# Strassen products for seven pairs of tiles, gated loads, another tile order and masks on VectorE in a fused attention and feed-forward kernel

## The chip, the cores and the metric

The kernel runs on one core of a Trainium2 chip. The metric is the device time of one execution in microseconds (us); the lower, the better. Times are medians of the runs of one batch. A run more than 1.5% above the fastest run of the same kernel is put down as slow and left out of the ratios.

## The reference

Local attention with a few global keys feeds a two-layer network. The shapes are batch 4, 8 heads, 768 positions, head size 64; 8 global keys and a local window of 96; model width 512, hidden width 2048.

```python
scores = scale * q @ k.T                              # per batch and head
keep = (key < 8) | ((rel >= 0) & (rel < 96))          # rel = query - key
dist = 96 where global and not local, else abs(rel)
a = softmax(where(keep, scores - slope[h] * dist, -1e9))
x = (a @ v) as [3072, 512]                            # heads side by side
h = x @ w_in                                          # [3072, 2048]
g = h - tanh(h)
out = g @ w_out                                       # [3072, 512], float32
```

Scores outside the local window vanish, so a tile of 128 queries needs its own 128 keys, the 128 before them and the 8 global ones. There are 4 x 6 = 24 tiles.

## The kernel before

A planner written in Python runs a list scheduling with assumed durations and fixes the order of the instructions on each engine before the kernel is built. It decides order only. At run time each instruction still waits for its real inputs, so a plan that guesses a landing too early makes an engine stand still at an instruction whose data is not there.

The first four tiles go alone, the other twenty in ten pairs. Work on one tile: keys and queries are turned on TensorE for the first tiles and by the crossbar transpose of the DMA engines later; scores (`a_S`), exponential on ScalarE (`a_E`), mask multiply on VectorE (`a_M`), attention times values (`a_AV`), normalisation on VectorE (`a_R`), another transpose, first layer (`m1`), tanh on ScalarE, subtraction on VectorE (`m1_g`), second layer (`m2`), eviction on ScalarE, store.

The parts that the change and the argument touch (cuts marked by `...`):

```python
tiles = [(u % B, u // B) for u in range(NU)]          # one tile of each batch in turn
...
def a_R(u, a):                                        # normalise, VectorE only
    ...
    nc.vector.reciprocal(rd, t[:, :, Dh : Dh + 1])
    nc.vector.tensor_tensor(out=x, in0=t[:, :, 0:Dh], in1=rd.to_broadcast([P, NP, Dh]), op=ALU.mult)
...
def m2(g, t, qq):                                     # 4 x 4 matmuls of 512 columns a tile
    ...
    for f in range(qq * 4, qq * 4 + 4):
        nc.tensor.matmul(o, gg[:, f, t * P : (t + 1) * P], w_out_bf[f // FJ][:, f % FJ, :],
                         start=(f == 0), stop=(f == CF - 1))
...
# identity and the distance maps on GpSimd, in its queue between the loads
pl.op(("dist", 1), POOL, 1.1, lambda e: build_dist(1), after=[("issue", ("ld", "k", 2))], pri=-2)
pl.op(("dist", 2), POOL, 1.1, lambda e: build_dist(2), after=[("issue", ("in", 1))], pri=-1.5)
pl.op(("ident",), POOL, 0.6, lambda e: make_identity(nc, ident), after=[("issue", ("ld", "k", 1))], pri=-3)
...
# the plan holds a load of tile u >= 6 back behind a block of the first layer (in the plan only)
go = [kk for a, kk in prog if a <= u - AHEAD - EARLIER] if u >= 6 else []
pl.op(key, POOL, 0.88, ..., after=[prev and ("issue", prev), go[-1] if go else None], dma=T_LD)
...
# all DMAs in one line; a crossbar transpose counts as landed 0.5 us later than another
d0 = max(dma_free, end + (1.2 if eng is SP else 1.5))
dma_free = d0 + o["dma"]
done[key] = dma_free + 0.7 + o["lag"]                 # lag=0.5 for the transposes
```

The softmax here doesn't subtract the row's maximum and nothing guards it: scores larger than these inputs give would overflow.

## Time and profile before

| quantity | before | how to read it |
|---|---|---|
| time | 217.93 us (217.9 to 218.61, 3 runs) | whole execution |
| span in the profile | 216.6 us (of another run, 218.34 us) | first to last instruction |
| TensorE busy | 205.0 us, 95% | not yet "at its peak": listed lengths overlap (a block of eight first-layer matmuls is listed at 1.04 us and takes 0.87) |
| VectorE / ScalarE busy | 60% / 57% | room for work moved off TensorE |
| useful TensorE work | 194.2 us | worked out in the prediction |

### The profile page before, as it was taken

The numbers are of one execution on the slowest core, as the hardware profiler recorded it, in microseconds if no ns is written. First come the engines' busy times: TensorE is split into PE (matmuls) and PEld (weight loads), VectorE is DVE, ScalarE is ACT, GpSimd is POOL, SyncE is SP. The second block draws the span as 40 slices with busy tenths as digits, with TensorE's granted clock in tenths as the row PEclk, the third lists the DMA queues.
The fourth block names the chain that finished last, engine by engine and source line by source line (L and its number), as shares of the span: only waits on it lengthen the run. The fifth ranks groups of instructions, "written<-read, shape, count | busy, mean of one in ns | idle before, by whom it ended". The sixth has DMA issues, their size and how long they took to land.

```text
span 216.6 us, 5328 instructions
## 1 busy us (share of the span) xinstructions
PE 205.0 (95%) x2095; PEld 143.9 (66%) x2121; DVE 130.1 (60%) x296; ACT 124.1 (57%) x244; POOL 69.8 (32%) x90
## 2 busy tenths in 40 slices
PE   8667999999999999999999999999999999999994
PEld 5446989455867857676676677667677667666643
DVE  2385868530797977777668568568557557333310
ACT  2694768422968576546745745745745745443421
POOL 7996356473625606331441341340000000000000
PEclk9999999999999999999999999999999999999999
DMA  9999999999999998999999999999523411201112
GB/s 126 125 146 195 188 200 184 182 148 165 236 132 160 182 150 129 142 146 149 124 149 159 116 118 144 114 142 134 108 65 77 111 39 49 73 3 48 48 48 97
DMA packets 111016, 27.34 MB, mean 126 GB/s; under 512 B 103696, under 2 KB 108048, under 8 KB 110992
## 3 DMA queue, kind: packets, MB, share of 16 engines
q0 software_dynamic: 77024, 13.37, 87.3%
q1 hardware_dynamic: 33968, 13.64, 33.6%
q8 instruction: 16, 0.26, 0.5%
q14 instruction: 8, 0.07, 0.1%
HBM read 27.26 MB, written 6.29 MB: 155 GB/s over the span
## 4 chain that ended last, share of the span: by engine, by line
PE 78%; DMA 15%; POOL 3%; issue 2%; ACT 0%; POOLq 0%
PE bank L339 33%; PE bank L382 33%; DMA qT<-qb 6%; DMA qb<-in_q_dram 5%; PE bank L282 5%; DMA w_in_bf<-in_moe_w_in_dram 3%; PE bank L303 2%; PE bank L301 2%; PE bank L362 2%; POOL vb L452 1%; PE bank L326 1%; POOL kb L452 1%; POOL qb L452 1%; POOL rmat L238 0%; POOL rmat L241 0%
## 5 line engine op out<-in xcount | busy, mean ns | idle before, releaser
L339 PE MATMUL bank<-xT,w_in_bf 128*128 128x256 bf16 (+1 forms) x896 | 97.6, 257 | 0.2 <-DVE xT L272 0.2
L382 PE MATMUL bank<-w_out_bf,g 128*128 128x512 bf16 x342 | 87.4, 379 | 1.5 <-issue 0.2
L542 ACT ACTIVATE th<-bank 128x512 f32<-128x512 f32 x96 | 56.2, 609 | 55.1 <-PE bank L339 50.8
L339 PEld LDWEIGHTS <-w_in_bf 128*128 128x128 bf16 x896 | 75.0, 98 | 17.5 <-issue 0.2
L348 DVE TENSOR_TENSOR g<-bank,th 128x512 bf16<-128x512 f32 x96 | 64.1, 687 | 31.7 <-ACT th L542 31.3
L382 PEld LDWEIGHTS <-g 128*128 128x128 bf16 x368 | 35.2, 98 | 28.3 <-DVE g L348 0.4
L452 POOL DMA_DIRECT2D kb<-in_k_dram x23 | 20.5, 891 | 50.5 <-DMA kT<-kb 25.4
L287 ACT ACTIVATE pd<-bank 128x512 bf16<-128x512 f32 x48 | 26.1, 601 | 8.4 <-PE bank L282 8.3
L452 POOL DMA_DIRECT2D qb<-in_q_dram x23 | 20.3, 882 | 17.8 <-DMA qT<-qb 3.9
L292 DVE TENSOR_TENSOR pd<-pd,mk 128x1024 bf16<-128x1024 bf16 x24 | 16.6, 692 | 13.6 <-ACT pd L287 13.5
L270 ACT COPY ot<-bank 128x512 f32<-128x512 f32 (+2 forms) x25 | 14.4, 574 | 18.1 <-PE bank L382 12.1
L452 POOL DMA_DIRECT2D vb<-in_v_dram x24 | 21.3, 890 | 5.1 <-PE bank L303 2.2
L287 ACT ACTIVATE po<-bank 128x512 bf16<-128x512 f32 x40 | 22.1, 622 | 0.0
L313 DVE TENSOR_TENSOR x<-bank,rden 128x256 bf16<-128x256 f32 x48 | 20.4, 425 | 1.7
L292 DVE TENSOR_TENSOR po<-po,mk 128x1024 bf16<-128x1024 bf16 x20 | 13.8, 692 | 5.2 <-ACT po L287 5.2
L282 PEld LDWEIGHTS <-kT 64*128 64x128 bf16 x352 | 10.1, 94 | 8.2 <-issue 7.8
L282 PE MATMUL bank<-qT,kT 64*128 64x128 bf16 x352 | 14.0, 217 | 0.6 <-DMA qT<-qb 0.5
L301 PE MATMUL bank<-vb,pd 128*128 128x65 bf16 x192 | 14.0, 193 | 0.1
L301 PEld LDWEIGHTS <-pd 128*128 128x128 bf16 x192 | 12.5, 97 | 2.1 <-DVE pd L292 0.4
L303 PE MATMUL bank<-vb,po 128*128 128x65 bf16 x160 | 12.4, 193 | 0.0
L303 PEld LDWEIGHTS <-po 128*128 128x128 bf16 x160 | 10.4, 97 | 1.7
L317 DVE COPY kT<-kT 128x32 bf16<-128x32 bf16 x16 | 4.5, 282 | 9.1 <-PE bank L282 8.8
(38 smaller groups left out, 73.6 us busy)
## 6 DMA issues: line engine op xcount, KB each, us to landing
out_dram<-ot SPq DMA_DIRECT2D x23, 256.0 KB, 3.3
vb<-in_v_dram POOLq DMA_DIRECT2D x24, 128.0 KB, 6.2
kb<-in_k_dram POOLq DMA_DIRECT2D x23, 128.0 KB, 7.3
qb<-in_q_dram POOLq DMA_DIRECT2D x23, 128.0 KB, 7.2
w_in_bf<-in_moe_w_in_dram POOLq DMA_DIRECT2D x4, 512.0 KB, 10.1
w_out_bf<-in_moe_w_out_dram POOLq DMA_DIRECT2D x4, 512.0 KB, 13.1
kT<-kb SPq DMA_TRANSPOSE x18, 5.7
qT<-qb SPq DMA_TRANSPOSE x18, 5.4
```

Of the source, the lines that this page charges most:

```text
L270: nc.scalar.copy(out=dst, in_=src)
L282: nc.tensor.matmul(t[hh][:, p * P : (p + 1) * P], kt[r, p, :], qt[r, p, :], start=True, stop=True)
L287: nc.scalar.activation(dst, t, AF.Exp, bias=0.0, scale=scale)
L292: nc.vector.tensor_tensor(out=p, in0=p, in1=mk[:, m, :, :], op=ALU.mult)
L301: nc.tensor.matmul(o, pd[:, slot(h), :], vd[:, h, :], start=True, stop=w is None)
L303: nc.tensor.matmul(o, buf("po", ("p", u, 1))[:, slot(h), :], bufs[vname(w)][got["vb", w]][:, h, :], start=False, stop=True,)
L313: nc.vector.tensor_tensor(out=x, in0=t[:, :, 0:Dh], in1=rd.to_broadcast([P, NP, Dh]), op=ALU.mult)
L339: nc.tensor.matmul(t[:, (f - f0) * n : (f - f0 + 1) * n], w_in_bf[j][:, c, fo : fo + P], xt[:, c, 0:n], start=(c == 0), stop=(c == CD - 1),)
L348: nc.vector.tensor_tensor(out=dst, in0=t.rearrange("q (b n) -> q b n", n=n), in1=th.rearrange("q (b n) -> q b n", n=n), op=ALU.subtract,)
L382: nc.tensor.matmul(o, gg[:, f, t * P : (t + 1) * P], w_out_bf[f // FJ][:, f % FJ, :], start=(f == 0), stop=(f == CF - 1),)
L452: pl.op(key, POOL, 0.88, lambda e, u=u, src=src, dst=dst: nc.gpsimd.dma_start(out=dst(), in_=rows(src, u)), after=[prev and ("issue", prev ...
L542: pl.op(("th", g, f), ACT, 0.55, lambda e, g=g, f=f: nc.scalar.activation(buf("th", ("th", g, f)), buf("bank", ("h", g, f)), AF.Tanh, bias ...
```

## The change

Its intent is to take work from TensorE, which is full. Seven pairs do the second layer by Strassen's scheme: seven half-size products in place of eight, at the price of sums on VectorE. The rest makes room for that and mends the plan.

```diff
+    FAST = set(range(6, 13))              # the pairs done by Strassen
+    def a_sum(e, g, kk):                  # 5 sums of 128x1024 bf16 a pair, VectorE
+        add(e, buf("hb", ("a", g, kk)), gblk(...), sign, gblk(...))
+    def product(g, kk):                   # one of seven: 8 matmuls of 256 columns
+        for f in range(CH):
+            ...
+            nc.tensor.matmul(o, a, b, start=(f == 0), stop=(f == CH - 1))
     ... ten sums of the output weights once; five steps of recombination a pair (s34 t u cx ab cs)
-    tiles = [(u % B, u // B) for u in range(NU)]
+    TILES = [(0, 0), (0, 1), (1, 0), (1, 1), (1, 2), (3, 0), ...]   # a batch's tiles follow each other
+    R_ENGS = [(ACT, 0.7), (DVE, 0.36)]    # normalisation may go to ScalarE, in 4 pieces of 64
     ... copies of the global keys and values too
-    pl.op(("ident",), POOL, 0.6, lambda e: make_identity(nc, ident), ...)
-    pl.op(("dist", 1), POOL, 1.1, ...)
+    pl.op(("rel",), POOL, 0.45, lambda e: build_rel(), ...)          # one iota
+    pl.op(("ident",), DVE, 0.2, ... tensor_scalar(out=ident, in0=rel, ... is_equal))
+    pl.op(("dist", 1), DVE, 0.6, ...)     # the maps from the iota, on VectorE
+                if go:
+                    gates[key] = go[-1]   # the gate becomes a real wait of the load
-              after=[("ld", nm, u), go], ..., dma=T_TR, lag=0.5)
+              after=[("ld", nm, u), go], ..., dma=T_TR, lag=LATE)    # LATE = 2.0
     ... the plan's DMA model: two rings that share the engines, in place of one line
+    arrive = "q1 k1 q2 v0 q3 k2 q0 v1 v2 i0 k3 i1 v3 i2 i3 v6 k5 v5 ...".split()
+    pl.op(("touch",), ACT, 0.5, ... dma_start(out=touch, in_=w_in_r[:, :, 0:16]))  # early small read
```

A gate is the block of the first layer behind which the plan holds a load back; from now on the load really waits for it. A bank is one of the eight pieces of the memory that TensorE writes its results to.

Some smaller edits came with these: keys and queries of seven tiles in place of six are turned on TensorE, and attention outputs of six in place of eight; values are stored 96 wide in place of 65; the scores of a tile are planned as two pieces; the lead of loads over the first layer in the plan is 4.5 tiles in place of 4.0; limits hold back how many banks each layer may take.

## The prediction

> **What bounds the kernel now.** I read the occupancy slices first, then the chain of waits, then the groups of instructions, and last the timelines of single engines, because a busy share alone would mislead here.
>
> ```profile
> span 216.6 us, 5328 instructions
> PE 205.0 (95%) x2095; PEld 143.9 (66%) x2121; DVE 130.1 (60%) x296; ACT 124.1 (57%) x244; POOL 69.8 (32%) x90
> PE   8667999999999999999999999999999999999994
> DVE  2385868530797977777668568568557557333310
> PEclk9999999999999999999999999999999999999999
> DMA  9999999999999998999999999999523411201112
> PE 78%; DMA 15%; POOL 3%; issue 2%; ACT 0%; POOLq 0%
> ```
>
> The reader is to see a TensorE that is full from the fifth slice (about 21 us) to the end at full clock, with VectorE at five to seven tenths beside it. DMA is busy for three quarters of the run, but its 15% of the chain lies mostly in the first 30 us. Whether "full" is also back to back is answered by the chain of waits in the middle of the run:
>
> ```profile
> 103.33 0.81 PE bank L382 x3
> 104.14 0.55 PE bank L282 x16
> 104.69 0.98 PE bank L339 x8
> 105.67 0.86 PE bank L382 x4
> 106.53 0.87 PE bank L339 x8
> 107.41 0.86 PE bank L382 x4
> ```
>
> The columns are start, length and work. Eight first-layer matmuls 256 wide take 0.87 us, four second-layer matmuls 512 wide 0.86 us, sixteen score matmuls 0.55 us, and each piece starts where the last ended. So the middle is bound by TensorE's issue rate, and only work taken from TensorE there shortens the run. The start is different (timeline of TensorE, then of GpSimd):
>
> ```profile
> 17.50 0.40 PE L326 MATMUL bank<-ident,kb 128*128 128x128 bf16 x4 [2.38 <-DMA kb<-in_k_dram]
> 17.73 1.06 PE L339 MATMUL bank<-xT,w_in_bf 128*128 128x128 bf16 x16
> 9.03 0.78 POOL L422 DMA_DIRECT2D w_in_bf<-in_moe_w_in_dram  x1
> ```
>
> The first weight block is issued at 9.03 and landed 7.54 us later, at 16.6 (chain of waits). The first matmul that uses it starts only at 17.73, because four transposes of a key tile stand ahead of it in the queue and their load lands at 17.50.
>
> Useful TensorE work of the kernel before, at issue intervals read from the trace: first layer 640 x 0.109 + 256 x 0.0557 = 84.0; second layer 368 x 0.2165 + last tile 3.5 = 83.2; scores 352 x 0.0345 = 12.1; attention times values 352 x 0.0295 = 10.4; transposes 80 x 0.056 = 4.5. Sum 194.2 us. Of the 217.9 us measured, some 24 us are therefore no useful matmul: 9.5 us waiting for first data between 5.1 and 17.7, 5.1 us before that, some 5 us of small gaps after 17.7, and about 4 us of last evictions, store and launch.
>
> **What the Trainium skill says.** (1) "TensorE: Matmul & The Clock Gate", section "Wait — 56ns, not 53.3ns?": warm matmuls start N / 2.4 GHz plus about 2.5 ns apart. For N = 256 that is 109 ns; the trace agrees (0.87 us for eight). Cutting a 512-wide matmul into two 256-wide ones thus costs almost nothing, and seven products instead of eight are a real eighth less. (2) "VectorE: DVE Perf Modes", section "The perf-mode tier table (the rule you actually need)": a two-tensor operation runs at 2x for bf16 in SBUF and at 1x with a PSUM or float32 operand. The trace agrees: 1024 bf16 elements take 692 ns, 512 float32 from PSUM 687 ns. (3) "Perfetto Trace Analysis", section "Optimizing Scalar/DVE Operations": the listed latency of an instruction is longer than the time it holds the engine. The trace agrees: six subtractions of 687 ns each took 3.67 us in a row, 0.60 us apart. I count VectorE by these distances: 0.60 for the subtraction, 0.61 for a mask multiply, 0.34 for a normalisation half, 0.19 for its reciprocal. (4) "ScalarE: Activation LUTs", section "What ACT_TABLE_LOAD costs": 186 ns plus 0.833 ns per element, 93 ns more for a pointer operand, 93 ns overlap. For 64 elements with a pointer scale that is 0.24 us apiece (an estimate from that page; no instruction of the kernel before has this form).
>
> **The change, part by part.** *Strassen.* Seven of the ten pairs of tiles do their second layer in seven products of eight 256-wide matmuls: 7 x 7 x 8 x 0.109 = 42.7 us in place of 14 x 16 x 0.2165 = 48.5 us. TensorE work falls by 5.8 us, to 188.4. All of it lies in the bound part, so it is the certain gain if nobody else holds TensorE up.
>
> What it costs VectorE: per pair five sums of 128x1024 bf16 (5 x 0.61), and for recombination one 256-wide SBUF sum (0.28, estimated from the 0.34 with PSUM), one 256-wide with PSUM (0.34), two 512-wide with PSUM (1.2) and one 512-wide in SBUF (0.58): 5.45 us. Seven pairs make 38, and ten once-only sums of the output weights 6. In return 27 of the 48 normalisation halves and 10 of the 16 value copies go to ScalarE in the built order, about 9 + 2 us. VectorE goes from 60% to some 75% of the span. ScalarE gains 108 small pieces x 0.24 = 26 us and loses 14 evictions of 0.5 us.
>
> An average is not enough, so I counted the tight stretch in the built order: VectorE from the first Strassen sum to the last reciprocal of attention. It holds 28 sums (17.1), 43 subtractions (25.8), 24 masks (14.6), 26 reciprocals (4.9), 12 normalisation halves (4.1), 25 recombinations (12.0), 11 small copies (2.6): 81 us. TensorE's order over the same stretch (from the first-layer block that feeds that sum to the last attention matmul) holds 45 blocks of 0.87 (39.2), 35 products (30.5), scores 6.6, attention 6.1 and second layer 4.3: 86.8 us. ScalarE has 46 tanh (25.3), 48 exponentials (23.5), 56 pieces (13.4) and some 5 of copies: 67 us. So TensorE stays the longest, but VectorE is at 94% in strict order. I charge 2 us for bubbles over about ten tiles.
>
> *Start.* GpSimd makes one iota (0.3) in place of the identity and two masks before the first weight issue (about 1.4 us in the chain of waits), but eight loads now precede the weights in its queue, where seven did (0.88 more). The issue comes about 0.2 us earlier. The small early read of the weights on ScalarE's queue may take a first-access delay off: between 12 and 13 us DMA's share drops to 0.87 from about 2, so I guess 0.5. More certain: first-layer matmuls now stand right behind the weights instead of behind the key transposes, and 17.73 can become about 16.1, 1.6 us. Before it stand 0.7 us more of attention work than before (32 score and 32 value matmuls, against 24 and 16). Together 2.2 us.
>
> *Gates and late landings in the plan.* In the trace before, TensorE waits for a crossbar transpose twice, 0.2 and 0.3 us (the long DMA pieces in the chain overlap other matmuls). At most 0.5 us is to be had. *Tile order* moves no TensorE work; its sole effect is in what is ready when.
>
> Sum: 217.9 - 5.8 - 2.2 - 0.5 + 2.0 = 211.4; I say 211.5.
>
> **The rivals.** *VectorE becomes the bound.* For it: 94% in the tight stretch by my count; if instructions run at their listed durations (0.69 instead of 0.60), 81 becomes 93 us and the stretch loses 6 us, which eats the gain: about 217. Against it: the runs of back-to-back subtractions in the trace do keep 0.60, and the seven-pair choice and the shift to ScalarE look made to keep VectorE below TensorE. *The start gains much more.* For it: 9.5 us lie idle there. If weights come through 4 us sooner, 208. Against it: the queue order still puts ten 128-row loads ahead of the first weight block, and the early DMA slices are full. *Chained latency at the bank limits.* Four first-layer banks and two product groups may be out at once; a product's banks come free only after a string of three to five VectorE steps. If each pair loses one such string, about 1 us, seven pairs give the whole gain back: about 216.
>
> **Range and chances.** The 5.8 us is firm arithmetic; the start (0 to 4) and the VectorE bubbles (0 to 6) are soft and partly cancel. That gives 207.5 to 214.5 at 8 in 10. The 2% line is at 213.6, and I put 0.79 on its faster side, 0.18 within and 0.03 slower, since even with VectorE bound the result is about even.
>
> **What would show it.** Right: the product groups at 0.87 us per eight matmuls, back to back; pairs during attention some 15.3 us apart instead of 16.2; first first-layer matmul at about 16; VectorE near 9 tenths in the middle slices without TensorE waiting for it for more than 2 us in all. Wrong: idle time of the weight loads of products put down to the sums, or of first-layer matmuls to the subtraction (then VectorE is the bound); a first weight landing later than 16.6 (then the eighth load cost more than the masks); new waits for crossbar transposes in the middle of the run.

## The result

The changed kernel took 211.87 us (median of four runs, 210.34 to 213.14) against 218.27 for the kernel before in the same batch (four runs, 217.9 to 219.37). The ratio is 0.9696, with a 95% interval of 0.9602 to 0.979. A ratio here is the mean time of one kernel's fast runs over that of the other's fast runs of the same rounds, so it is not quite the ratio of the medians quoted. The profiled run took 213.13 us. A second profile, of the unaltered kernel in the first batch of experiments, comes from a run of 210.33 us; I use both, since where they disagree a reading isn't safe.

The page of the changed kernel (the 213.13 run): span, busy times, three rows of slices, then the shares of the chain that ended last.

```profile
span 211.3 us, 5806 instructions
PE 200.9 (95%) x2276; PEld 160.5 (76%) x2287; DVE 159.8 (76%) x349; ACT 144.3 (68%) x352; POOL 68.1 (32%) x83
PE   6988999999999999999979999999999999999993
DVE  6693878894195554988868999998999889898610
PE 61%; DMA 22%; POOL 7%; ACT 4%; issue 2%; DVE 2%; ACTq 0%; POOLq 0%
```

TensorE is still full, with one visible notch in the twenty-first slice (106 to 111 us). VectorE rose to 76%, where some 75% was predicted, and reads eight to nine tenths from 111 to some 195 us. The share of DMA in the chain went from 15% to 22%, which invites the reading that the kernel has become bound by transfers. The same line of the other profile of the same kernel forbids it:

```profile
PE 91%; DMA 5%; DVE 1%; POOL 1%; issue 0%; ACT 0%; POOLq 0%
```

One execution's chain steps through whichever wait was nearest and then follows a transfer backwards while TensorE works on. Its shares differ by 17 points between two runs of one program that are 1.3% apart. I read the stretches instead.

The chain in the middle of the run (213.13 run; start, length, work):

```profile
147.63 0.55 PE bank L393 x16
148.18 0.98 PE bank L328 x8
149.16 0.87 PE bank L457 x8
150.03 0.87 PE bank L328 x8
```

Line 328 is the product, line 457 the first layer, line 393 the scores. Eight product matmuls take 0.87 us, and each piece starts where the last one ended, as before the change. The clearest sign of what Strassen brings is the distance between the score matmuls of every second tile, which is the time of one pair. First the kernel before, then the one after (timeline of TensorE; start, length, instruction):

```profile
112.16 0.62 PE L282 MATMUL bank<-qT,kT 64*128 64x128 bf16 x16
...
128.34 0.62 PE L282 MATMUL bank<-qT,kT 64*128 64x128 bf16 x16
```

```profile
124.91 0.62 PE L393 MATMUL bank<-qT,kT 64*128 64x128 bf16 x16
...
140.30 0.62 PE L393 MATMUL bank<-qT,kT 64*128 64x128 bf16 x16
...
155.69 0.62 PE L393 MATMUL bank<-qT,kT 64*128 64x128 bf16 x16
```

A pair took 128.34 - 112.16 = 16.18 us and now takes 15.39 us, twice in a row. The saving of 0.79 us a pair is close to the eighth of the second layer that it should be (5.8 / 7 = 0.83).

To see the whole run I counted the useful TensorE work in three stretches (the weight loads of each kind, times the distance at which such matmuls start, as in the prediction) and took it from the elapsed time. What is left is TensorE's idle time, good to about 1 us. (Up to 50 us all first-layer matmuls of the kernel before are 128 wide; of the 272 of the kernel after, 16 are 256 wide.)

| idle TensorE, us | 0 to 50 | 50 to 110 | 110 to last matmul | last matmul at |
|---|---|---|---|---|
| before (218.34 run) | 16.1 | 1.9 | 1.5 | 213.7 |
| after, 213.13 run | 13.9 | 4.4 | 1.4 | 208.1 |
| after, 210.33 run | 12.4 | 2.8 | 1.4 | 205.3 |

So the end lost nothing although VectorE is much busier there, the start gained 2.2 to 3.7 us, and the middle lost 0.9 to 2.5 us. These are the waits of the middle (213.13 run, timeline of TensorE, in the last row of VectorE; the bracket is the idle time before the group and who ended it):

```profile
78.59 1.91 PE L457 MATMUL bank<-xT,w_in_bf 128*128 128x256 bf16 x16 [0.42 <-DMA xT<-x]
...
96.00 1.05 PE L457 MATMUL bank<-xT,w_in_bf 128*128 128x256 bf16 x8 [0.40 <-DMA xT<-x]
...
109.52 0.62 PE L393 MATMUL bank<-qT,kT 64*128 64x128 bf16 x16 [1.23 <-DVE ot L302]
108.13 0.69 DVE L466 TENSOR_TENSOR g<-bank,th 128x512 bf16<-128x512 f32 x1 [1.05 <-ACT th L700]
```

Two are crossbar transposes that landed late. The third is the notch: scores wait for a VectorE sum that empties a bank of products. That sum reads products that TensorE made just before (from 107.25 us), and VectorE itself had sat idle for 1.05 us shortly before it (last row). So it was late by this chain of steps and not for want of VectorE time. It fits the prediction's rival of chained latency at the banks, but the other profile does not have it; that one waits 1.35 us for a query transpose at 90.85 us instead.

At the start, the first first-layer matmul begins at 16.00 us where it began at 17.73. GpSimd issues the weights as follows (213.13 run; line 559 is the first-layer weights, the last row holds the third and the fourth piece), after the one line of the kernel before that holds its third and fourth piece:

```profile
14.12 1.51 POOL L422 DMA_DIRECT2D w_in_bf<-in_moe_w_in_dram  x2
```

```profile
8.43 0.82 POOL L559 DMA_DIRECT2D w_in_bf<-in_moe_w_in_dram  x1
...
11.68 1.59 POOL L559 DMA_DIRECT2D w_in_bf<-in_moe_w_in_dram  x2
```

The first piece is issued only 0.6 us sooner than before (9.03), but the last two are issued 2.4 us sooner. They land at 23.75 and 26.29 us, where they landed at 24.63 and 27.20, so 0.9 us sooner; in the 210.33 run, with the same issue times within 0.1 us, at 22.26 and 24.80, 2.4 us sooner.

### The profile page after: what moved, and what is told of

It reads as the page before. It is cut to its first block, busy times and chain, and to the rows that moved or that the text cites. A ratio compares the mean times of both kernels' runs of the same rounds, so it can differ in the third digit from the quotient of the medians.

```text
span 211.3 us, 5806 instructions
## 1 busy us (share of the span) xinstructions
PE 200.9 (95%) x2276; PEld 160.5 (76%) x2287; DVE 159.8 (76%) x349; ACT 144.3 (68%) x352; POOL 68.1 (32%) x83
## 4 chain that ended last, share of the span: by engine, by line
PE 61%; DMA 22%; POOL 7%; ACT 4%; issue 2%; DVE 2%; ACTq 0%; POOLq 0%
PE bank L457 28%; PE bank L328 20%; DMA xT<-x 7%; DMA w_in_bf<-in_moe_w_in_dram 7%; DMA kb<-in_k_dram 5%; PE bank L498 5%; DMA out_dram<-ot 4%; PE bank L393 3%; POOL vb L591 2%; POOL qb L591 2%; PE bank L414 2%; PE bank L479 2%; PE bank L412 2%; POOL kb L591 1%; POOL w_in_bf L559 1%
## 5 line engine op out<-in xcount | busy, mean ns | idle before, releaser
L457 PE MATMUL bank<-xT,w_in_bf 128*128 128x256 bf16 (+1 forms) x896 | 95.7, 257 | 1.4 <-DMA xT<-x 0.8
L466 DVE TENSOR_TENSOR g<-bank,th 128x512 bf16<-128x512 f32 x80 | 53.2, 681 | 9.0 <-ACT th L700 8.9
L328 PEld LDWEIGHTS <-hb 128*128 128x128 bf16 x280 | 27.1, 98 | 3.1
L429 ACT ACTIVATE x<-bank,rden 128x64 bf16<-128x64 f32 x108 | 23.6, 317 | 2.4 <-DVE rden L421 2.3
L302 DVE TENSOR_TENSOR hb<-g 128x1024 bf16<-128x1024 bf16 x35 | 22.8, 681 | 0.1
L403 DVE TENSOR_TENSOR pd<-pd,mk 128x1024 bf16<-128x1024 bf16 x24 | 16.5, 688 | 8.1 <-ACT pd L398 8.1
L328 PE MATMUL bank<-bsum,hb 128*128 128x256 bf16 x168 | 21.6, 273 | 0.0
L498 PE MATMUL bank<-w_out_bf,g 128*128 128x512 bf16 x72 | 18.5, 379 | 0.4
L381 ACT COPY ot<-bank 128x512 f32<-128x512 f32 (+2 forms) x11 | 6.2, 561 | 13.5 <-PE bank L498 7.2
L328 PE MATMUL bank<-bsum,g 128*128 128x256 bf16 x112 | 14.5, 273 | 0.0
L328 PE MATMUL bank<-w_out_bf,hb 128*128 128x256 bf16 x112 | 14.5, 273 | 0.0
```

Source lines behind the costliest of these rows:

```text
L302: eng_of(e).tensor_tensor(out=out, in0=x, in1=y, op=ALU.add if sign > 0 else ALU.subtract)
L328: nc.tensor.matmul(o, a, b, start=(f == 0), stop=(f == CH - 1))
L403: nc.vector.tensor_tensor(out=p, in0=p, in1=mk[:, m, :, :], op=ALU.mult)
L429: nc.scalar.activation(x[:, h, :], t[:, h, 0:Dh], AF.Copy, bias=0.0, scale=rd[:, h, :])
L457: nc.tensor.matmul(t[:, (f - fa) * n : (f - fa + 1) * n], w_in_bf[j][:, c, fo : fo + P], xt[:, c, 0:n], start=(c == 0), stop=(c == CD - 1),)
L466: nc.vector.tensor_tensor(out=dst, in0=t.rearrange("q (b n) -> q b n", n=n), in1=th.rearrange("q (b n) -> q b n", n=n), op=ALU.subtract,)
```

## The experiments

Twelve kernels ran, in three batches on three chips, five rounds each. All gave correct results. The first is the kernel after itself; each of the others changes one thing of it, the run with the gates from tile 7 on two. "Over the kernel after" below means: the difference of its ratio and that of the unaltered repeat (0.9682, first batch), times 218 us. Each ratio's interval is about 0.003 to 0.006 to either side, so such a difference is good to about 1 us, and less than that is not told apart. The unaltered kernel ran in the first batch only. For the other two batches this takes its ratio to be the same on their chips; two edits of the second batch that were meant to make it slower came out 0.9 and 1.2 us below it, so that may be off by about 1 us.

**The kernel after, unaltered** (no edit), to see the spread that the four first runs left open.

> The changed kernel itself, unaltered, as the base of this study. Its first four times were two near 210.5 us and two near 213.1 us. If that is the chance of single executions, the ten or so times here should again fall into two groups 2 to 3 us apart. If it was something of that one chip, they should lie within 1 us.

Six fast runs from 210.33 to 211.88 us, median 211.22 against 218.19; ratio 0.9682 (0.965 to 0.9713). The two groups of the first batch (210.5 and 213.1) did not come back. What made them is open.

**No Strassen pairs.**

```diff
-    FAST = set(range(6, 13))
+    FAST = set()
```

> The changed kernel with no pair in seven products: all ten pairs do their second layer in plain 512-wide matmuls, the rest stays. Theory A (TensorE bounds, VectorE has room): the full 5.8 us of TensorE work come back, less about 1 us of bubbles between 60 and 110 us that hang on the products, so 4.5 to 6 us over the changed kernel, about 216.5 us. Theory B (VectorE at its limit beside attention eats most of the saving): under 3 us over it. Rival C (the gain is mostly the start and the plan): under 1.5 us over it.

216.01 us, ratio 0.9896 (0.9859 to 0.9934): 4.7 us over the kernel after. VectorE falls to 57% of the span. The first theory, that the products bring nearly their full count, holds. The other half of the expectation, that 1 us of bubbles in the middle hangs on the products, does not: without any product TensorE is idle for 2.7 us between 50 and 110 us, as in the repeat (2.8). The same run tells the rest: all other parts together bring 218 x (1 - 0.9896) = 2.3 us.

**Only the last two of the seven pairs.**

```diff
-    FAST = set(range(6, 13))
+    FAST = {11, 12}
```

> The changed kernel with only the two pairs in seven products whose products run after attention has ended. Theory A (each pair is worth 0.83 us wherever it stands): 7 to 2 pairs gives up 4.1 us, so 3.5 to 4.5 us over the changed kernel. Theory B (only the pairs outside attention pay): within 1 us of the changed kernel.

Ratio 0.9875 (0.9828 to 0.9921) from five runs (213.88 to 216.85; the profiled run, 220.22 at a granted clock of 0.984, was slow and is not read): 4.2 us over the kernel after. Five pairs given up cost 0.84 us each. The idea that only the last pairs pay, because the early ones are eaten by waits, falls.

**One pair more.**

```diff
-    FAST = set(range(6, 13))
+    FAST = set(range(5, 13))
```

> The changed kernel with an eighth pair in seven products, the one before the seven (tiles 6 and 7). Theory A (TensorE bounds, VectorE has room, as the run with all normalisation on VectorE showed): 0.83 us less TensorE work, 0.3 to 0.9 us faster. Rival: so early the ten weight sums and these products stand in VectorE's queue at 40 to 70 us, where it is behind, and hold TensorE: 0.5 us slower or more.

212.22 us, ratio 0.9717 (0.969 to 0.9745): 0.8 us over the kernel after where 0.3 to 0.9 less was expected. The direction is on the rival's side, but the intervals overlap. In its profile TensorE's idle time between 50 and 110 us is 4.5 us, against 2.8 us in the repeat, but the other profile of the unaltered kernel has 4.4, so where the pair's 0.83 us went is not shown. Nothing here speaks for an eighth pair.

**All normalisation on VectorE**, to load VectorE further in the stretch where my count had it at 94%.

```diff
-    R_ENGS = [(ACT, 0.7), (DVE, 0.36)]
+    R_ENGS = [(DVE, 0.36)]
```

> The changed kernel with all 48 normalisation halves on VectorE, none on ScalarE: 27 halves x 0.34 us = 9 us more for VectorE, about 4.8 us of it in the tight stretch where the trace shows it 90 to 95% busy over 75 us, so some 6 us idle. Theory A (room, but not much): 1 to 4 us slower than the changed kernel, with TensorE waiting for VectorE. If VectorE has ample room: within 0.7 us. Theory B (already at its limit): 4 us slower or more.

211.93 us, ratio 0.9708 (0.9677 to 0.9739): 0.6 us over the kernel after: the expectation's case of ample room (within 0.7 us), and not the 1 to 4 us thought likelier. The table of stretches shows it (columns: from:to and length, then busy us of TensorE, its weight loads, VectorE, ScalarE, GpSimd, each with its count; granted clock, DMA share, GB/s). The kernel before, the repeat, and this experiment:

```profile
110.00:170.00 60.00, 59.53 (x588) 41.04 (x595) 38.71 (x83) 35.47 (x67) 12.97 (x15) 1.00 1.09 120
```

```profile
110.00:170.00 60.00, 60.00 (x724) 52.36 (x722) 55.26 (x114) 44.74 (x110) 18.48 (x21) 1.00 1.27 131
```

```profile
110.00:170.00 60.00, 59.90 (x717) 51.92 (x716) 57.28 (x123) 35.89 (x68) 18.42 (x21) 1.00 1.25 133
```

VectorE goes from 38.7 to 55.3 and to 57.3 of 60 us, and TensorE stays at 59.9 to 60.0. Over the whole run VectorE gained 7.9 us of work, but in this stretch only 2.0 us (4.8 were expected for the tight stretch), so the step tested is from 92% to 95%. Even there VectorE does not hold TensorE up. The likely reason, not tested, is that the plan puts VectorE's work in an order in which each result is needed some time after it is made. The 0.6 us is within what isn't told apart.

**Without the real gates.**

```diff
-                if go:
-                    gates[key] = go[-1]
```

> The changed kernel without the gates: the loads of tiles 6 and up are issued in the same order, but GpSimd's queue no longer waits for the first-layer matmul that the plan names, only for free buffers. The prediction gave gates and late landings together at most 0.5 us, so within 0.7 us of the changed kernel (211.2). Rival: with loads running ahead, the crossbar transposes share the 16 engines with more queued loads and land later, so TensorE waits for them between 50 and 110 us: 1.5 us slower or more.

213.69 us, ratio 0.9776 (0.9733 to 0.982): 2.0 us over the kernel after. The sums of TensorE's waits by releaser (total us, times, longest), for the repeat and then for this experiment:

```profile
PE bank L393 <- DMA qT<-qb: 1.4, 1, 1.4
```

```profile
PE bank L393 <- DMA qT<-qb: 4.3, 5, 1.2
```

Scores wait for query transposes five times in place of once, 2.9 us more. The query transposes landed later too. From issue to landing, repeat first:

```profile
DMA to landing us min/median/max: 2.4/4.1/7.9
```

```profile
DMA to landing us min/median/max: 2.4/5.8/8.5
```

The stretch from 50 to 110 us (columns as above; the DMA column can pass 1), repeat first, shows what went on meanwhile:

```profile
50.00:110.00 60.00, 58.65 (x631) 43.35 (x630) 41.16 (x91) 45.17 (x109) 18.43 (x21) 1.00 1.41 145
```

```profile
50.00:110.00 60.00, 56.73 (x608) 41.77 (x614) 39.13 (x88) 43.81 (x107) 23.70 (x27) 1.00 1.85 155
```

GpSimd issues 27 loads there in place of 21, and the share of DMA goes from 1.41 to 1.85. So the rival fits: ungated loads run ahead of the plan, the transposes that are needed now share the engines with them, and they land later. (The kernel before, without real gates, has 28 instructions, 1.77 and a median landing of 5.4 us.)

**Landings as optimistic as before.**

```diff
-    LATE = 2.0
+    LATE = 0.5
```

> The changed kernel planned with crossbar landings 0.5 us after the transfer, as before, in place of 2.0. The prediction gave at most 0.5 us to gates and late landings together. The run without gates already lost about 2 us to late transposes, so the theory is now that TensorE's fixed order must allow for late landings: 0.7 to 2 us slower, with waits of the score matmuls for query transposes between 50 and 110 us. If the late landings in the plan do nothing: within 0.4 us.

Ratio 1.0114 (1.0059 to 1.017): 9.4 us over the kernel after, and slower than the kernel before, where 0.7 to 2 was expected. The profiled run was slow (225.23 us, clock 0.985), so its lengths are not compared, but what it waits for is plain:

```profile
PE bank L393 <- DMA qT<-qb: 10.8, 6, 3.7
```

```profile
148.34 0.62 PE L393 MATMUL bank<-qT,kT 64*128 64x128 bf16 x16 [3.68 <-DMA qT<-qb]
```

Six score blocks stand still for 10.8 us in all, 3.7 us at the worst. In the repeat the query transposes land 2.4 to 7.9 us after they are issued, 4.1 in the median. The kernel before planned with the same 0.5 and waited 0.5 us in all.

Its plan did not expect later landings: the planners are plain Python and run without a chip, and for the tiles from 9 on they put a median of 9.7 us between the issue of a query load and its scores in the kernel before, 9.7 in this one and 11.1 with 2.0. What differs is the loads. From 60 us on, a query load had landed 19.5 us before its transpose was issued in the kernel before (median of 14, each load matched with its transpose) and 18.6 us in the run without gates, but 0.05 us in the repeat and 0.13 us here. With real gates a late load is thus a late transpose. For the wait of 3.68 us the load was issued at 135.36 us and landed at 143.01, its transpose was issued at 143.06 and landed at 148.20. So the 2.0 seems to be needed because the loads are gated. That is read from traces and not tested: the old landing time without gates did not run.

**Masks on GpSimd again.** The identity and the distance maps are made as in the kernel before, between the loads (the code of the section on the kernel before, put back).

```diff
-    pl.op(("rel",), POOL, 0.45, ...)  and ("ident",), ("dist", m) on DVE
+    pl.op(("ident",), POOL, 0.6, ...)
+    pl.op(("dist", 1), POOL, 1.1, ...)
+    pl.op(("dist", 2), POOL, 1.1, ...)
```

> The changed kernel with the identity and the masks made on GpSimd again, between the loads, as before the change. The first weights are then issued about 1.4 us later (the five small operations in the chain of waits before). If the start is bound by that queue: first first-layer matmul 1 to 1.4 us later than about 16, and 0.7 to 1.4 us slower. If the start is bound by the transfers themselves: under 0.4 us.

Ratio 1.0094 (1.0051 to 1.0137): 9.0 us over the kernel after, where 0.7 to 1.4 was expected. GpSimd's timeline shows a wait that nobody had foreseen. The load at the head of its second batch, first in the repeat, then here:

```profile
19.05 0.89 POOL L591 DMA_DIRECT2D vb<-in_v_dram  x1 [5.76 <-PE bank L457]
```

```profile
26.67 0.89 POOL L592 DMA_DIRECT2D vb<-in_v_dram  x1 [11.01 <-PE bank L460]
```

This load, the values of tile 6, has a real gate: a block of the first layer of the tile at place 1. That tile needs the second map, which GpSimd makes last; so this plan does the tile third. The gate opens 7.6 us later, and behind it in the same queue stand the other loads and the output weights, which TensorE then lacks:

```profile
40.02 1.90 PE L501 MATMUL bank<-w_out_bf,hb 128*128 128x512 bf16 x7 [1.35 <-DMA w_out_bf<-in_moe_w_out_dram]
```

**The same with the gates from tile 7 on**, which frees that one load and tells the gate's cost from the masks' cost.

```diff
 (as above, and)
-    GATE = 6
+    GATE = 7
```

> The run with the masks on GpSimd again, but with the gate taken off the one load that heads the second batch of loads (values of tile 6). In that run's trace this load waited 11 us, until 26.7, for the first first-layer matmul of tile 1, which comes late because tile 1 needs the mask that GpSimd builds last; all later loads and the output weights stood behind it. Theory: that gate, and not the mask work, made the 9.8 us. Then this run falls back to 212 to 214.5, the later start alone. Rival: the mask work itself (GpSimd's queue, later attention) costs it: 218 or more still.

214.7 us, ratio 0.983 (0.9798 to 0.9862). The gate made 5.8 of the 9.0 us; masks on GpSimd by themselves cost 3.2 us over the kernel after. GpSimd issues the weights as follows:

```profile
10.10 0.77 POOL L560 DMA_DIRECT2D w_in_bf<-in_moe_w_in_dram  x1
...
14.33 1.51 POOL L560 DMA_DIRECT2D w_in_bf<-in_moe_w_in_dram  x2
```

The first piece is 1.6 us later than in the repeat (8.51), the last two 2.6 us (11.75). TensorE's idle time up to 50 us is 16.5 us against 12.4, so 4.1 us more; between 50 and 110 us it is 1.3 us less (1.5 against 2.8), after that 0.9 us more. Together that is the 3.7 us between the two profiled runs (214.0 and 210.33 us).

**The old order of arrival.**

```diff
-    arrive = "q1 k1 q2 v0 q3 k2 q0 v1 v2 i0 k3 i1 v3 i2 i3 v6 k5 v5 q5 k4 q4 o0 v4 o1 o2 q6 k0 k6 o3".split()
+    arrive = "k0 q0 k1 q1 v0 v1 k2 q2 v2 i0 k3 q3 v3 i1 i2 i3 k4 q4 v4 o0 o1 k5 q5 v5 o2 o3".split()
```

> The changed kernel with the loads in the order of before: seven in front of the first weight block instead of eight, three more in front of the second instead of one. My reckoning of the start (1.6 us from first-layer matmuls standing right behind the weights, 0.7 us from more attention work ahead of them) says that order gives most of the start's gain: 1 to 2.2 us slower. Rival: the start is bound by bytes, and the order hardly matters: within 0.5 us.

210.41 us, ratio 0.9629 (0.9584 to 0.9674), not slower at all. It is the lowest ratio, but its interval overlaps that of the repeat, which ran on another chip; it beats the kernel before and is not told apart from the kernel after. Its first first-layer matmul starts at 13.98 us, two us sooner than in the repeat, yet the second group starts only at 17.30 (17.70 in the repeat), and TensorE's idle time is 13.5 us up to 50 us and 1.7 from there to 110, against 12.4 and 2.8: no difference in the sum. Here the early first matmul was worth nothing, since the next ones did not follow.

**Without the early read of the weights.**

```diff
-    pl.op(("touch",), ACT, 0.5, lambda e: nc.scalar.dma_start(out=touch, in_=w_in_r[:, :, 0:16]), pri=-9)
```

> The changed kernel without the small early read of the first-layer weights on ScalarE's queue. The prediction guessed 0.5 us for it: the first weight block lands 0.5 us later, so 0.3 to 0.7 us slower. If that guess was empty: within 0.2 us, or a little faster.

211.91 us in the median, ratio 0.9643 (0.9593 to 0.9693) from four runs. A fifth run, 212.91 us at a granted clock of 1.000, was left out by the 1.5% rule. No loss is seen: the read does nothing that these runs can show.

**The old order of the tiles.**

```diff
-    TILES = [(0, 0), (0, 1), (1, 0), ...]
+    TILES = []
```

> The changed kernel with the tiles in the old order (one tile of each batch in turn). The prediction said the tile order moves no TensorE work: within 1 us of the changed kernel (211.2). Rival: the order decides what is ready in the first 50 us or how crossbar landings fall, and is worth 1.5 us or more either way.

Inconclusive. Two runs of six count as fast (210.42 and 212.01 us), the others lie between 214.03 and 216.9, and there is no ratio. One of these others ran at a granted clock of 0.999, so part of the spread may be this kernel's own. The fast ones lie in the range of the kernel after, so no gain from the tile order is shown, and none is excluded in the mean.

## Why the prediction was right or wrong

The time came out where the prediction had it: 211.87 us for 211.5, inside the range. Step by step it is less even.

*Strassen, 5.8 us: right.* The pairs are 15.39 us apart, where 15.3 was predicted and 16.18 was before. From 110 us on, TensorE's idle time is as small as before. Taking all seven pairs away costs 4.7 us with about 1 us of doubt, taking five away 4.2. The 4.7 is 1.1 us under the 5.8, about the doubt.

*VectorE bubbles, 2.0 us: the size was about right, the place and the cause were wrong.* The step that failed is the charge of 2 us "over about ten tiles" because VectorE is at 94% in strict order (81 of 86.8 us is 93%; the trace has it 92% busy from 110 to 170 us). In that stretch TensorE lost nothing, even when the experiment took VectorE to 57.3 of 60 us. What idle time came up (0.9 to 2.5 us) lies between 50 and 110 us. In one profile it holds two waits for crossbar transposes (0.8 us) and one for a bank that a VectorE sum freed late (1.23 us), in the other one wait for a query transpose (1.35 us). As a whole it does not hang on the products either: without any, the middle has 2.7 us. New waits for transposes in the middle were on the prediction's own list of what would show it wrong. A count of busy time in strict order says whether an engine can keep up, not that it will be late. The rival "VectorE becomes the bound" falls with it (its "about 217" doesn't follow from the sum either: 6 us of bubbles in place of 2.0 make 215.4). Of the rival "chained latency at the bank limits" (a loss of 1 us a pair) the traces show one case in one of two runs.

*Start, 2.2 us together: about right in size (2.2 and 3.7 us in the two profiles), wrong in its parts.* The 2.2 doesn't follow from its own terms: 0.2 + 0.5 + 1.6 - 0.7 is 1.6. The first first-layer matmul did come at 16.00 us, as said. But the step "first-layer matmuls right behind the weights, 1.6 us" rests on one instruction: with the old arrival order it comes at 13.98 us and the run is no different. The 0.5 us for the early read was a guess and is not there (the view's DMA share before the dip was 1.49, not about 2). The masks, which I netted to 0.2 us, are the part that the experiments show at work: 3.2 us if put back. The term was mis-sized because I followed the first weight piece only, which was issued 0.6 us sooner, and put both masks before it. GpSimd's timeline has the second map behind the second piece, and the third and fourth piece were issued 2.4 us sooner. No run moves the second map alone, so that it was these pieces is argued.

*Gates and late landings, at most 0.5 us: wrong in kind.* I read their worth from the waits of the kernel before. There they could have saved little. In the new plan they are what keeps the other parts' gain: without gates 2.0 us are lost, with the old landing time 9.4. The step that failed is the reading of the two as small and separate: with gates a transpose is issued 0.05 us after its load lands (19.5 us after it in the kernel before), so a real gate takes away the slack that had hidden a late load. Nor did the waits for transposes shrink; they went from 0.5 us to 0.8 in one profile and 1.4 in the other.

*The sum.* Undoing single parts loses 4.7, 2.0, 9.4 and 9.0 us, and the whole change gained 6.9 (1 - 0.9682 of 218). The parts are not additive: a plan, its gates and its landing times fit each other, and two of them, each put back alone (the old landing time, the masks on GpSimd), give a kernel slower than the kernel before. That the right sum came out is partly luck, as the start's terms, the bubbles' place and the gates' worth show.

## What to carry to other kernels

Here work taken from the bound engine came through almost in full with the helper engine 92 to 95% busy, so test the helper's room by loading it more, and don't charge a loss for a high busy share alone. Judge a start by the bound engine's idle time over the whole fill and by the last pieces of the data, not by the moment of the first useful instruction. Before a real wait is put into an in-order queue of loads, ask what stands behind it and which event opens it: here a shift of that event by 7.6 us moved all that followed. And a wait that holds loads back also uses up the slack behind them, so plan later landings with it.

## What the Trainium skill lacked or had wrong

- How late a crossbar transpose lands beside other queued loads. "DMA: Bandwidth & Descriptors", section "DMA Transpose (X-bar)", gives the constraints but no landing time. Here query transposes of 128x512 bf16 landed 2.4 to 7.9 us after issue, 4.1 in the median (5.8 without gates), and planning with 0.5 in place of 2.0 us of lag cost 9.4 us beside gated loads.
- What a wait at the head of GpSimd's queue of loads costs the loads behind it. No page that I used has it. The runs show 11.0 us of wait in place of 5.8, and 5.8 us of run time between the two settings of the gate.
- The estimate of 0.24 us for a ScalarE piece of 64 elements with a pointer scale, from "ScalarE: Activation LUTs", section "What ACT_TABLE_LOAD costs", was a little high: eight took 1.67 us in a row in the repeat. One is listed at 0.31 us (first row below), so they came (1.67 - 0.31) / 7 = 0.19 us apart.

```profile
L429 ACT ACTIVATE x<-bank,rden 128x64 bf16<-128x64 f32 x108 | 23.4, 313 | 2.1 <-DVE rden L421 2.0
```

```profile
127.34 1.67 ACT L429 ACTIVATE x<-bank,rden 128x64 bf16<-128x64 f32 x8
```

- The chain of waits as a view: two profiles of one kernel gave DMA 22% and 5% of it. No page that I used warns of it.
